# Two weight blocks split earlier, in the spatial weight's rooms, and one group's request moved ahead of three stores

## The chip, the cores and the metric

The kernel runs on one core of one Trainium2 chip. The metric is device time in microseconds (us) for one execution. Each shown time is one execution of the whole program.

## The reference

Inputs are q, k, v of shape 4 x 8 x 768 x 64 (batch, heads, positions, head width). First a retention layer with a decay per head, then a gated MLP with a spatial weight, everything in float32:

```python
gamma = 1.0 - 2.0 ** (-5.0 - np.arange(H))
for t in range(S):
    state = gamma * state + np.einsum('bhd,bhe->bhde', k[:, :, t], v[:, :, t])
    y[:, :, t] = np.einsum('bhd,bhde->bhe', q[:, :, t], state) / np.sqrt(D)
x = y.transpose(0, 2, 1, 3).reshape(B, S, H * D)          # 4 x 768 x 512
h = np.maximum(x @ w_in, 0.0)                             # w_in: 512 x 1024
u, v = h[..., :512], h[..., 512:]
v_n = (v - mean(v)) / np.sqrt(var(v) + 1e-06)             # over the last axis
v_s = np.einsum('ts,bsd->btd', w_spatial, v_n) + b_spatial[None, :, None]
out = (u * v_s) @ w_out                                   # w_out: 512 x 512
```

The weights w_in and w_out arrive as 64-bit floats; w_spatial is 768 x 768.

## The kernel before

**Tiling.** The positions of each batch make six groups of 128, so 24 groups in all, numbered from 0 (groups 0 to 5 are batch 0). Group g is three DMA requests: two for its values and queries (tile qv) and one for its keys (kk). Both tiles have three buffers, so group g can be requested when the last reader of group g - 3 is done. Retention runs per group: scores `s`, outputs `x`, then `xf` (scaled, VectorE), `xh` (rounded high part, ScalarE) and `xl` (the rest, GpSimd). The MLP of a batch has six tiles V (one per group: products `v`, activation `vr`, statistics `bst`, `mv`, `rs`, `nb`, normalised `vnh`), and eight units (four column blocks j, two halves of the positions). A unit has products `u`, activation `ur`, the spatial product `sp`, the gate `t` (two VectorE steps, L542 and L543), `gh` (ScalarE), `gl` (GpSimd), and the output product `o`. Accuracy comes from products of high and low parts, so each float32 weight needs a high and a low half.

**Weight blocks.** The 64-bit weights are twelve blocks of 128 x 512, split on the chip. Blocks 0 to 3 are V's weight, 4, 5, 6 and 8 are u's weight for j = 0, 1, 2, 3, and blocks 7, 9, 10, 11 are w_out for j = 0 to 3. A split is: `split_top` (ScalarE, L184, writes a), `split_exponent` (two VectorE steps on a, L190, L192), `split_sign` (two VectorE steps, L201 writes f, L205 writes a), `split_low` (one VectorE step, L210), `split_high` (ScalarE, L213, the high half), `split_residue` (two GpSimd steps, L140 and L227, the low half). In the profile a and f are `da` and `df`, or `room` where they lie in the spatial weight's buffers: four rooms of the pool tag "wsp" serve as a for blocks 0 to 5 before the last three tiles of the spatial weight (wst3 to wst5) take them.

**Order.** Nothing here is reordered freely: `START`, `FIRST` and the strings after them are lists of words that `emit` carries out one by one (L34 to L52), and each engine works off its own instructions in that order. Letters: a top, c the three VectorE steps (c60 is block 6, step 0), H high, R residue, C all of a split, V products of a V tile, r its activation, s statistics, w power, n bias, N normalise, u and D products u, P spatial product, O output product, I a whole unit, S scores and state of a group, Z scores alone, X its output, G request of a group, L request of a weight block, K request of a spatial tile, W its split. All requests and stores are issued by one queue, SyncE's (SP), which handles them strictly in turn; an issue whose buffer is not free holds up all behind it.

**The place of the change** is batch 0's MLP, about 56 to 125 us of the profile. PSUM tag "m" has two buffers, shared by `v`, `u` and `sp`; a buffer is handed on in the order in which its last reader was written in the list. In `START` the word `u1` stands ahead of `r4`, and `u0` ahead of `r5`; so V tile 5 gets the buffer of u1 and the first `sp` that of u0. Blocks 6 and 7 are split only in `FIRST` (`C6 P0 C7 P1`), after tile 5 of V.

Of the kernel before, what the change touches and what calls it, by code (L numbers as in the profile page):

```python
# [9 lines left out]
F32 = mybir.dt.float32  # L10
# [28 lines left out]
)  # L39
FIRST = (  # L40
    "C6 P0 C7 P1 D2 O0 C8 C9 P2 G7 Z5 D3 O1 C10 P3 S6 D4 O2 G8 C11 X6 S7 I4 G9 X7 S8 W0 G10 I5 X8 "
    "S9 W1 G11 I6 X9 S10 W2 G12 V0 V1 I7 X10 S11 G13 N0 V2 N1 V3 N2 X11 G14 V4 N3 V5 N4 O7 N5"
)
SECOND = (
    "S0 I0 W3 X0 S1 G3 I1 W4 X1 S2 G4 I2 W5 X2 S3 G5 I3 X3 S4 G6 I4 X4 S5 G7 I5 X5 G8 "
# [10 lines left out]
STAGED = {i: (("vnh", "vnl")[i // 3], i % 3) for i in range(6)}  # L56
STAGED |= {i: ("vnl", i - 8) for i in range(8, 11)}
UNIT_BLOCKS = 2
WARM_UP = 10


@with_exitstack
def tile_retention_gmlp(
# [17 lines left out]
    P = 128  # L81
# [8 lines left out]
    DM = KT * P  # L90
# [8 lines left out]
    mpool = ctx.enter_context(tc.tile_pool(name="mlp", bufs=2))  # L99
# [75 lines left out]
    def sp_tile(dtype, name):  # L175
        return mpool.tile([P, 2, HALF], dtype, tag="wsp", name=name, bufs=2 * (NC // 2) + 1)

    rooms = [sp_tile(F32, f"room{i}").rearrange("p i c -> p (i c)")[:, :DM] for i in range(4)]
# [15 lines left out]

    def split_sign(i):
        a, _, parts = halves[i]
        f = mpool.tile([P, DM], F32, tag="u", name=f"df{i}", bufs=3)[:, :]
        halves[i][1] = f
        ai, fi = a.bitcast(I32), f.bitcast(I32)
        tc.keep_in_program_order(  # L200
            nc.vector.scalar_tensor_tensor(  # L201
                fi, parts[:, :, 1], -0x40000000, ai, ALU.bitwise_and, ALU.bitwise_or
            )
        )
        tc.keep_in_program_order(nc.vector.tensor_scalar(ai, fi, -0x800000, None, ALU.bitwise_and))  # L205
# [9 lines left out]
    def split_residue(i):  # L215
        hi, lo, _ = doubles[i]
        a, f, _ = halves.pop(i)
        if i < UNIT_BLOCKS:

# [12 lines left out]
    def split_double(i):  # L232
        for step in (split_top, split_exponent, split_sign, split_low, split_high, split_residue):
            step(i)
# [339 lines left out]
    def item(b, i):  # L574
# [40 lines left out]
        "u": lambda b, g, n: mlp_u(0, *units[n]),  # L615
        "a": lambda b, g, n: split_top(n),
        "c": lambda b, g, n: (split_exponent, split_sign, split_low)[n % 10](n // 10),
        "H": lambda b, g, n: split_high(n),
        "R": lambda b, g, n: split_residue(n),
# [9 lines left out]
    wps = ps_o.tile([P, DM], F32, tag="o", name="wps")  # L629
    for i in range(WARM_UP):  # L630
        nc.tensor.matmul(wps, wz[:, :P], wz, start=True, stop=True)
# [84 lines left out]
```

## Time and profile before

| | |
|---|---|
| times of three runs | 417.2, 421.4, 425.0 us (median 421.4) |
| the profiled execution | 420.8 us, its span 418.8 us |
| TensorE busy | 387.2 us, 92% of the span |
| VectorE, GpSimd, ScalarE busy | 53%, 37%, 31% |
| mean granted TensorE clock | 0.976 |

TensorE is the busy engine. The rows to look for are therefore the stretches where it is not busy, or where its granted clock is below 1: each row of a wait names what released the engine, and each row of the windows gives busy time per engine and the clock (PEclk).

### The profile page before, as it was taken

Reading aid. Unit: us, or ns where it says so; the run is one execution under the profiler, and the core shown is the slowest. Engines: PE = TensorE matmul, PEld = TensorE weight load, DVE = VectorE, ACT = ScalarE, POOL = GpSimd, SP = SyncE. Lnnn points to the kernel's source line nnn. Section 1 sums busy time; section 2 is a strip of 40 time slices with the busy share of each in tenths; the row PEclk is TensorE's granted clock in tenths of the full one; section 3 lists DMA queues with packets and bytes.
Section 4 is the critical chain, followed back from the end, with each engine's and each line's share of the span. In section 5 each row is a group of like instructions: output and inputs, shape, how many; then the busy total and the mean of one; then the engine's idle time right before and its main releaser. Section 6 shows DMA issues by size and latency. Waiting matters only on the chain.

```text
span 418.8 us, 9002 instructions
## 1 busy us (share of the span) xinstructions
PE 387.2 (92%) x3748; PEld 327.6 (78%) x3748; DVE 222.0 (53%) x505; ACT 131.8 (31%) x242; POOL 156.3 (37%) x152
## 2 busy tenths in 40 slices
PE   4877999599939999999999999999999999999996
PEld 1546776367728777799999988899998988999995
DVE  0999763886925676557666224575553245212122
ACT  2464534222230233643223223721113135411212
POOL 0476851766640445225444412334442321011010
PEclk9989999779987999999999999999999999999999
DMA  7979959100071333323346410133302000200202
GB/s 181 320 241 257 295 182 294 43 2 2 2 226 52 102 102 99 103 77 103 107 121 189 130 38 2 68 102 108 105 2 77 0 2 0 77 0 1 77 1 75
DMA packets 14392, 41.47 MB, mean 99 GB/s; under 512 B 2320, under 2 KB 2704, under 8 KB 14352
## 3 DMA queue, kind: packets, MB, share of 16 engines
q1 hardware_dynamic: 14352, 40.91, 32.7%
q8 instruction: 29, 0.48, 0.5%
q14 instruction: 11, 0.09, 0.1%
HBM read 34.61 MB, written 6.29 MB: 98 GB/s over the span
## 4 chain that ended last, share of the span: by engine, by line
PE 84%; DMA 7%; POOL 3%; SPq 2%; DVE 2%; issue 1%; ACT 1%; POOLq 0%; DVEq 0%; ACTq 0%
PE sp L132 25%; PE u L132 17%; PE o L132 16%; PE v L132 15%; PE x L132 5%; PE s L132 5%; DMA qv<-in_qv_dram 4%; DMA kk<-in_k_dram 3%; SPq L137 2%; POOL qv L276 1%; POOL xl L140 1%; DVE xf L398 1%; POOL df L140 0%; POOL wout_w L227 0%; POOL winu_w L227 0%
## 5 line engine op out<-in xcount | busy, mean ns | idle before, releaser
L140 POOL TENSOR_TENSOR gl<-t,gh 128x384 fp32r<-128x384 f32 x31 | 32.4, 1044 | 132.1 <-ACT gh L544 74.5
L132 PE MATMUL u<-xh,winu_w 128*128 128x384 f32 x256 | 73.8, 351 | 2.4 <-POOL winu_w L227 2.4
L132 PE MATMUL o<-wout_w,gh 128*128 128x512 f32 x192 | 62.8, 408 | 3.4 <-POOL wout_w L227 3.4
L542 DVE TENSOR_TENSOR t<-sp,bsp_t 128x384 f32<-128x384 f32 (+1 forms) x34 | 18.0, 533 | 83.1 <-PE sp L132 83.1
L132 PE MATMUL v<-winv_w,xh 128*128 128x512 f32 x192 | 60.5, 397 | 0.6 <-ACT ur L511 0.6
L276 POOL TENSOR_TENSOR qv<-qv,vd_t 64x512 f32<-64x512 f32 x48 | 52.1, 1086 | 22.1 <-DMA qv<-in_qv_dram 20.3
L132 PEld LDWEIGHTS u<-xh,winu_w 128*128 128x128 f32 x256 | 47.9, 192 | 4.5 <-POOL winu_w L227 2.7
L132 PE MATMUL sp<-wsp_h,vnl 128*128 128x384 f32 x144 | 48.2, 335 | 0.0
L132 PE MATMUL sp<-wsp_h,vnh 128*128 128x384 f32 x144 | 48.2, 335 | 0.0
L132 PE MATMUL sp<-wsp_l,vnh 128*128 128x384 f32 x144 | 48.2, 335 | 0.0
L544 ACT CAST gh<-t 128x384 fp32r<-128x384 f32 (+1 forms) x34 | 16.6, 493 | 94.1 <-DVE t L543 93.8
L132 PEld LDWEIGHTS o<-wout_w,gh 128*128 128x128 f32 x192 | 36.6, 192 | 11.0 <-POOL wout_w L227 4.0
L132 PE MATMUL u<-xl,winu_w 128*128 128x384 f32 x128 | 43.8, 342 | 0.0
L140 POOL TENSOR_TENSOR xl<-xf,xh 128x512 fp32r<-128x512 f32 x24 | 31.4, 1309 | 31.5 <-ACT xh L415 31.4
L132 PEld LDWEIGHTS v<-winv_w,xh 128*128 128x128 f32 x192 | 35.4, 188 | 8.5 <-ACT ur L511 0.9
L320 DVE TENSOR_TENSOR qv<-s,mask_t 64x256 f32<-64x256 f32 x96 | 40.3, 419 | 1.6
L132 PE MATMUL s<-qv,kk 64*64 64x64 f32 x1296 | 26.9, 230 | 15.2 <-DMA kk<-in_k_dram 15.2
L132 PEld LDWEIGHTS s<-qv,kk 64*64 64x64 f32 x1296 | 23.5, 141 | 20.7 <-issue 11.8
L398 DVE SCALAR_TENSOR_TENSOR xf<-x,qg_t,qd_t 128x128 f32<-128x128 f32 x96 | 27.1, 342 | 23.0 <-PE x L132 22.9
L132 PE MATMUL o<-wout_w,gl 128*128 128x512 f32 x96 | 38.4, 400 | 0.0
L132 PE MATMUL v<-winv_w,xl 128*128 128x512 f32 x96 | 37.7, 392 | 0.8 <-POOL xl L140 0.8
L462 DVE BATCH_NORM_STATS2 bst<-vr 128x6 f32<-128x512 f32 x24 | 16.6, 692 | 33.1 <-ACT vr L455 33.1
(71 smaller groups left out, 569.5 us busy)
## 6 DMA issues: line engine op xcount, KB each, us to landing
qv<-in_qv_dram SPq DMA_DIRECT2D x48, 256.0 KB, 4.9
kk<-in_k_dram SPq DMA_DIRECT2D x24, 512.0 KB, 5.7
out_dram<-ot SPq DMA_DIRECT2D x23, 256.0 KB, 2.0
wst<-in_w_sp_dram SPq DMA_DIRECT2D x6, 384.0 KB, 8.2
raw<-in_w_inv_dram SPq DMA_DIRECT2D x4, 512.0 KB, 9.2
raw<-in_w_inu_dram SPq DMA_DIRECT2D x4, 512.0 KB, 9.6
raw<-in_w_out_dram SPq DMA_DIRECT2D x4, 512.0 KB, 6.8
bsp_t<-in_b_sp_dram SPq DMA_DIRECT2D x1, 384.0 KB, 10.9
```

The costliest lines, as they stand in the source:

```text
L132: ins = nc.tensor.matmul(out, lhs, rhs, start=start, stop=stop, skip_group_check=shared)
L137: tc.keep_in_program_order(nc.sync.dma_start(dst, src))
L140: return eng.tensor_tensor(out, whole, high.bitcast(F32), ALU.subtract)
L276: tc.keep_in_program_order(nc.gpsimd.tensor_tensor(w, w, vd, ALU.mult))
L320: keep(nc.vector.tensor_tensor(m[r][ROWS[r], i], ts[i][col, 0], mk, ALU.mult))
L398: nc.vector.scalar_tensor_tensor(xf[:, hp], t[:, hp].rearrange("p i c -> p (i c)"), qg_t[:, c, hp : hp + 1], qd_t[:, hp], ALU.mult, ALU.mult,)
L462: keep(nc.vector.bn_stats(st, norm[b, c][0]))
L542: nc.vector.tensor_tensor(t[:, c], pp[:, c], bsp_t[:, tc_], ALU.add)
L544: nc.scalar.copy(gh[:, c], t[:, c])
```

## The change

The change edits the two lists and the room for one tile. Nothing is computed differently: the same instructions run on every engine, 353 rows on VectorE and 228 on ScalarE in both.

```diff
     "t41 k41 l2 j5 y40 h3 t50 w1 y41 k50 s0 l3 V2 E4 w0 n1 h4 n0 c40 N1 l4 y50 r2 c41 V3 N0 s2 H4 "
-    "c42 y51 w2 r3 V4 E5 R4 L8 L9 L10 L11 K3 K4 K5 s3 h5 n2 u1 r4 l5 N2 s4 w3 V5 w4 n3 N3 n4 N4 u0 "
-    "r5 s5 w5 n5 N5"
+    "c42 y51 w2 r3 V4 E5 R4 L8 L9 L10 L11 s3 h5 a6 n2 r4 l5 N2 c60 u1 s4 w3 V5 w4 n3 N3 n4 N4 c61 "
+    "c62 H6 a7 c70 r5 u0 s5 R6 w5 n5 N5 c71 c72 H7 R7"
 )
 FIRST = (
-    "C6 P0 C7 P1 D2 O0 C8 C9 P2 G7 Z5 D3 O1 C10 P3 S6 D4 O2 G8 C11 X6 S7 I4 G9 X7 S8 W0 G10 I5 X8 "
-    "S9 W1 G11 I6 X9 S10 W2 G12 V0 V1 I7 X10 S11 G13 N0 V2 N1 V3 N2 X11 G14 V4 N3 V5 N4 O7 N5"
+    "C8 P0 G7 P1 G8 K3 K4 K5 C9 D2 O0 Z5 P2 D3 O1 C10 P3 S6 D4 O2 C11 X6 G9 S7 I4 X7 S8 W0 G10 I5 "
+    "X8 S9 W1 G11 I6 X9 S10 W2 G12 V0 V1 I7 X10 S11 G13 N0 V2 N1 V3 N2 X11 G14 V4 N3 V5 N4 O7 N5"
 )
...
+
+FAR = [6, 7]
...
     def split_sign(i):
         a, _, parts = halves[i]
-        f = mpool.tile([P, DM], F32, tag="u", name=f"df{i}", bufs=3)[:, :]
+        if i in FAR:
+            f = rooms[i - FAR[0]]
+        else:
+            f = mpool.tile([P, DM], F32, tag="u", name=f"df{i}", bufs=3)[:, :]
```

Blocks 6 and 7 are now split among the last two tiles of V; their a lies in rooms 2 and 3, their f in rooms 0 and 1, so wst3 to wst5 are requested after them (K3 to K5 moved into `FIRST`, behind groups 7 and 8). The activations r4 and r5 stand ahead of u1 and u0. The second spatial product P2 follows the scores Z5 instead of preceding them. The request of group 9 (G9) stands right behind X6. Line numbers below 60 grow by 2 and those after the new lines by 5.

The queue of SP, from the last weight block on (wst: spatial weight, qv and kk: a group, out: the stores of batch 0's first half). Before:

```order
L137 DMA wst3_737<-in_w_sp_dram 128x768
L137 DMA wst4_739<-in_w_sp_dram 128x768
L137 DMA wst5_741<-in_w_sp_dram 128x768
L137 DMA qv7_938<-in_qv_dram 64x1024 x2
L137 DMA kk7_939<-in_k_dram 128x1024
L137 DMA qv8_1084<-in_qv_dram 64x1024 x2
L137 DMA kk8_1085<-in_k_dram 128x1024
L569 DMA out_0_dram<-ot0_0_0_1202 128x512
L569 DMA out_0_dram<-ot0_0_1_1208 128x512
L569 DMA out_0_dram<-ot0_0_2_1214 128x512
L137 DMA qv9_1217<-in_qv_dram 64x1024 x2
L137 DMA kk9_1218<-in_k_dram 128x1024
```

Changed:

```order
L139 DMA qv7_862<-in_qv_dram 64x1024 x2
L139 DMA kk7_863<-in_k_dram 128x1024
L139 DMA qv8_881<-in_qv_dram 64x1024 x2
L139 DMA kk8_882<-in_k_dram 128x1024
L139 DMA wst3_886<-in_w_sp_dram 128x768
L139 DMA wst4_888<-in_w_sp_dram 128x768
L139 DMA wst5_890<-in_w_sp_dram 128x768
L139 DMA qv9_1122<-in_qv_dram 64x1024 x2
L139 DMA kk9_1123<-in_k_dram 128x1024
L574 DMA out_0_dram<-ot0_0_0_1203 128x512
L574 DMA out_0_dram<-ot0_0_1_1209 128x512
L574 DMA out_0_dram<-ot0_0_2_1215 128x512
```

Groups 7 and 8 went ahead of the three spatial tiles, and group 9 went ahead of the three stores.

ScalarE, from the last `xh` of batch 0 (group 5) to the last `vnh`. Before:

```order
L415 CAST xh3_578<-xf5_724 128x4x128
L511 ACTIVATE ur0_1_0_765<-u0_1_0_752 128x384
L455 ACTIVATE vr0_4_767<-v0_4_711 128x512
L485 ACTIVATE vnh0_448<-vr0_2_673,nb0_2_750,rs0_2_694 128x512
L485 ACTIVATE vnh0_448<-vr0_3_709,nb0_3_792,rs0_3_745 128x512
L485 ACTIVATE vnh0_448<-vr0_4_767,nb0_4_795,rs0_4_773 128x512
L511 ACTIVATE ur0_0_0_811<-u0_0_0_798 128x384
L455 ACTIVATE vr0_5_813<-v0_5_778 128x512
L485 ACTIVATE vnh0_448<-vr0_5_813,nb0_5_822,rs0_5_817 128x512
```

Changed:

```order
L420 CAST xh3_578<-xf5_724 128x4x128
L186 ACTIVATE room2_90<-raw6_86 128x512
L460 ACTIVATE vr0_4_747<-v0_4_711 128x512
L490 ACTIVATE vnh0_448<-vr0_2_673,nb0_2_745,rs0_2_694 128x512
L516 ACTIVATE ur0_1_0_766<-u0_1_0_753 128x384
L490 ACTIVATE vnh0_448<-vr0_3_709,nb0_3_789,rs0_3_739 128x512
L490 ACTIVATE vnh0_448<-vr0_4_747,nb0_4_792,rs0_4_770 128x512
L218 CAST winu_w_83<-room0_88 128x512
L186 ACTIVATE room3_91<-raw7_87 128x512
L460 ACTIVATE vr0_5_802<-v0_5_775 128x512
L516 ACTIVATE ur0_0_0_817<-u0_0_0_804 128x384
L490 ACTIVATE vnh0_448<-vr0_5_802,nb0_5_828,rs0_5_821 128x512
```

Each `vr` now stands ahead of the `ur` beside it, and block 6's top and high half and block 7's top lie between them.

VectorE, around the statistics of V tile 5 (bst0_5). Before:

```order
L462 BN_STATS bst0_5_815<-vr0_5_813 128x6
L463 BN_AGGR mv0_5_816<-bst0_5_815 128x2
L464 TENSOR_SCALAR rs0_5_817<-mv0_5_816 128x1
L474 TENSOR_SCALAR nb0_5_822<-mv0_5_816,rs0_5_817 128x1
L190 TENSOR_SCALAR da6_825<-da6_825 128x512
L542 TENSOR_TENSOR t0_0_0_843<-sp0_0_0_836,bsp_t_79 128x384
L192 TENSOR_SCALAR da6_825<-da6_825 128x512
L543 TENSOR_TENSOR t0_0_0_843<-t0_0_0_843,ur0_0_0_811 128x384
L201 SCALAR_TENSOR_TENSOR df6_829<-raw6_86,da6_825 128x512
L205 TENSOR_SCALAR da6_825<-df6_829 128x512
L210 SCALAR_TENSOR_TENSOR da6_825<-raw6_86,da6_825 128x512
L190 TENSOR_SCALAR da7_850<-da7_850 128x512
```

Changed:

```order
L206 SCALAR_TENSOR_TENSOR room0_88<-raw6_86,room2_90 128x512
L210 TENSOR_SCALAR room2_90<-room0_88 128x512
L215 SCALAR_TENSOR_TENSOR room2_90<-raw6_86,room2_90 128x512
L192 TENSOR_SCALAR room3_91<-room3_91 128x512
L194 TENSOR_SCALAR room3_91<-room3_91 128x512
L467 BN_STATS bst0_5_819<-vr0_5_802 128x6
L468 BN_AGGR mv0_5_820<-bst0_5_819 128x2
L469 TENSOR_SCALAR rs0_5_821<-mv0_5_820 128x1
L479 TENSOR_SCALAR nb0_5_828<-mv0_5_820,rs0_5_821 128x1
L206 SCALAR_TENSOR_TENSOR room1_89<-raw7_87,room3_91 128x512
L210 TENSOR_SCALAR room3_91<-room1_89 128x512
L215 SCALAR_TENSOR_TENSOR room3_91<-raw7_87,room3_91 128x512
```

Block 6 and the first two steps of block 7 went ahead of these statistics (block 6's own first two steps even ahead of tile 4's), and the rest of block 7 stands right behind them. The gate `t0_0_0` of the first unit then follows the two exponent steps of block 8.

## The prediction

> **What bounds the kernel now.** I read the waits of TensorE first, then the chain that ended last, then the windows. TensorE is busy for 92% of the span, so time can come only from where it stands still or runs at a lower clock. Its waits between 56 and 135 us (total, times, longest):
>
> ```profile
> PE s L132 <- DMA kk<-in_k_dram: 6.8, 1, 6.8
> PE o L132 <- POOL wout_w L227: 3.4, 1, 3.4
> PE u L132 <- POOL winu_w L227: 2.4, 1, 2.4
> PE v L132 <- ACT ur L511: 0.6, 1, 0.6
> PE sp L132 <- ACT ur L511: 0.6, 1, 0.6
> ```
>
> All five are in batch 0's MLP. Two are for the low halves of blocks 6 (winu_w) and 7 (wout_w), two for a PSUM buffer that `ur` gives back, and one for the keys of group 9. The chain gives start, length and work:
>
> ```profile
> 58.40 2.12 PE u L132 x12
> 61.08 3.02 PE v L132 x12
> 66.79 4.40 PE sp L132 x12
> 92.52 0.62 PE s L132 x32
> 97.52 3.87 PE sp L132 x12
> 101.39 1.09 PE s L132 x64
> 102.48 2.28 PE u L132 x12
> 104.77 2.08 PE o L132 x9
> 106.84 1.23 PE x L132 x32
> 115.31 2.09 PE o L132 x9
> 117.40 1.11 PE x L132 x32
> 119.77 5.27 DMA kk<-in_k_dram
> 125.28 2.10 PE s L132 x62
> 127.38 3.49 PE u L132 x12
> ```
>
> The last rows show what a wait costs beyond itself: after it, `s` took 2.10 us and `u` 3.49 us, against 1.09 and 2.28 at 101.39 and 102.48. The windows say why (length; busy us and instructions of PE, PEld, DVE, ACT, POOL; PEclk, DMA share, GB/s):
>
> ```profile
> 20.74:24.15 3.41, 1.34 (x22) 0.89 (x20) 3.32 (x8) 2.38 (x6) 1.83 (x2) 1.00 1.04 351
> 24.15:27.56 3.41, 3.41 (x18) 1.29 (x19) 3.38 (x7) 1.24 (x3) 3.00 (x4) 0.50 1.02 264
> 37.80:41.22 3.42, 2.04 (x38) 1.78 (x39) 3.24 (x9) 1.58 (x3) 1.19 (x2) 1.00 1.04 241
> 75.35:78.76 3.41, 1.02 (x6) 0.97 (x6) 3.38 (x4) 0.00 (x0) 2.31 (x2) 1.00 0.02 7
> 78.76:82.17 3.41, 2.23 (x7) 1.62 (x6) 2.27 (x6) 2.08 (x4) 2.14 (x2) 0.50 0.01 2
> 82.17:85.58 3.41, 1.17 (x3) 0.98 (x4) 3.31 (x4) 0.64 (x2) 2.19 (x2) 0.50 0.00 0
> 85.58:89.00 3.42, 3.42 (x9) 2.50 (x8) 3.27 (x4) 0.57 (x1) 2.92 (x2) 0.50 0.02 5
> ```
>
> The clock changes at steps of 3.41 us. A step with TensorE busy for 1.34 or 1.02 us is followed by clock 0.50; one with 2.04 us is not. It is back after a fully busy step, so the two gaps at 75 and 81 us halve the clock for three steps, to 89.00.
>
> **Part one: blocks 6 and 7 earlier, and the buffers.** From 58.40 to 101.39 the profile took 42.99 us. TensorE's work there at full clock is u 2 x 2.12, v 3.02, sp 4 x 3.87, u 2 x 2.28, o 2 x 2.08 and s 0.62: 32.08 us. So 10.91 us are the most that this part can give. They are 0.56 and 0.57 before `v` and `sp` (from chain rows to chain rows: 61.08 - 58.40 - 2.12, and likewise at 66.79), 0.53 inside the first `sp` (4.40 - 3.87), the waits of 2.4 and 3.4, and 3.4 of half clock, the remainder.
>
> The two buffer waits: V tile 5 now takes the buffer that `vr` of tile 4 frees, the first `sp` that of `vr` of tile 5. Each is a step done long before the next product asks, if ScalarE and VectorE keep up. They have the room:
>
> ```profile
> 61.55 0.69 DVE L462 BATCH_NORM_STATS2 bst<-vr 128x6 f32<-128x512 f32 x1 [3.71 <-ACT vr L455]
> 67.26 0.69 DVE L462 BATCH_NORM_STATS2 bst<-vr 128x6 f32<-128x512 f32 x1 [3.73 <-ACT vr L455]
> 69.40 0.81 ACT L485 ACTIVATE vnh<-vr,nb,rs 128x512 f32<-128x512 f32 x1 [2.17 <-DVE nb L474]
> ```
>
> A block is five VectorE steps, 0.43 + 0.43 + 0.69 + 0.43 + 0.69 = 2.7 us when GpSimd is idle, so two blocks want 5.3 of the 7.4 us in these two gaps. But GpSimd is not idle. Rows with it:
>
> ```profile
> 81.68 0.43 DVE L190 TENSOR_SCALAR da<-da 128x512 f32<-128x512 f32 x1 [1.07 <-ACT da L184]
> 72.49 0.69 DVE L201 SCALAR_TENSOR_TENSOR df<-raw,da 128x512 int32<-128x512 int32 x1
> 75.12 1.49 DVE L190 TENSOR_SCALAR da<-da 128x512 f32<-128x512 f32 x1
> 76.65 1.37 DVE L192 TENSOR_SCALAR da<-da 128x512 int32<-128x512 int32 x1
> 57.44 1.29 POOL L227 TENSOR_TENSOR winu_w<-df,room 128x512 fp32r<-128x512 f32 x1
> 74.65 1.68 POOL L140 TENSOR_TENSOR df<-df,winu_w 128x512 f32<-128x512 f32 x1 [0.45 <-DVE da L205]
> 76.41 1.33 POOL L227 TENSOR_TENSOR winu_w<-df,da 128x512 fp32r<-128x512 f32 x1
> ```
>
> L190 at 75.12 ends 0.28 us after the GpSimd step of 74.65 to 76.33, and L192 at 76.65 ends 0.28 after that of 76.41 to 77.74: such a step runs between two of GpSimd's, not beside them. I walk the new order with that rule.
> - Block 6's exponent steps start at 57.9 and, behind two GpSimd steps (57.44, and the `xl` that ends near 60), are done at 60.4. Tile 4's statistics follow at once, earlier than 61.55.
> - Block 6's other steps fit before 63.7. Block 7's exponent steps meet block 6's two residue steps and end at 66.8; tile 5's statistics start then. Before, `vnh` was done 2.95 us after their start (67.26 to 70.21); with nothing else in that chain now, it is done at 69.4 to 69.7. The first `sp`, which starts at 58.40 + 2.12 + 3.02 + 2.12 = 65.66, asks for it 5/6 x 3.87 later, at 68.9: 0.5 us of wait stay.
> - Second `sp` ends at 73.9. Block 6 is long done, so `u` has no wait: it ends at 76.2.
> - The first gate `t` stands behind the rest of block 7 and block 8's exponent steps, which run between block 7's residues: it starts at 73.2, is done at 74.8, `gh` at 75.3. On GpSimd, `gl` stands behind block 8's first residue step, which waits for block 8's high half and loses turns to VectorE: 75.7 to 76.9; `gl`, again between VectorE steps, ends at 78.4. The first `o` has used `gh` up by 76.7: 1.7 us of wait.
> - From there blocks 8 and 9 are done (79.6, 85.2) before `u` and the second `o` ask (84.5, 86.8), and TensorE runs to the end of the fourth `sp`. Block 10 (near 93) is asked for at 96.
>
> What stays is 0.5 + 1.7 = 2.2 us, so part one gives 10.9 - 2.2 = **8.7 us**. Bounds: 10.9 if nothing stays; below, the GpSimd waits of 2.4 and 3.4 could stay whole with their half clock of 3.4, leaving only the two buffer waits, 1.1. I take the walk, because it is made of rows. The 1.7 us lie between the two kinds of step seen above (1.34 busy of 3.41 lowers the clock, 2.04 of 3.42 does not): 3.41 - 1.7 leaves 1.7 busy. If that lowers it, one step at half speed costs another 1.7.
>
> The Trainium skill ("TensorE: Matmul & The Clock Gate", under "What's actually happening") says that the clock falls after at least one idle window of about 3.4 us. By that the stall would cost itself alone; the row at 20.74 disagrees, since 1.34 us of work did not save the clock.
>
> Moving P2 behind the scores costs nothing: `s` (0.62 us) is work that must be done anyway.
>
> **Part two: group 9 ahead of the stores.** SP's rows:
>
> ```profile
> 116.65 1.78 SPq L569 DMA_DIRECT2D out_dram<-ot  x3
> 118.60 1.12 SPq L137 DMA_DIRECT2D qv<-in_qv_dram  x2
> 119.77 0.58 SPq L137 DMA_DIRECT2D kk<-in_k_dram  x1
> ```
>
> The stores could go only when the first half's outputs were ready, and group 9 stood behind them. Its buffers are free once `x` of group 6 is done, at 106.84 + 1.23 = 108.07. From its first issue to the landing of kk passed 119.77 + 5.27 - 118.60 = 6.4 us. So it lands 6.4 us after `x6` ends, and the products that need it come s 1.09, u 2.28, sp 3.87, o 2.09, x 1.11 = 10.4 us after that end: 4 us to spare. The wait of 6.8 goes, and with it the half clock after it: 2.10 - 1.09 + 3.49 - 2.28 = 2.2. That is **9.0 us**. Bounds: 9.0 above, since TensorE has nothing else to lose there; below 6.8, if some other pause keeps a slow step. Next in line is group 10, behind the three stores and behind `x7`; it has the same 10.4 us against 6.4. The issues that were moved behind block 7's residues, wst3 to wst5, go out by about 73; the landing of such a tile
>
> ```profile
> wst<-in_w_sp_dram SPq DMA_DIRECT2D x3, 384.0 KB, 8.0
> ```
>
> puts them at 81, and the half that reads them began at 111.44, now about 103. That cover is 20 us; without it each us would show. Groups 7 and 8 go earlier, to no one's harm: nothing else is asked for before 81.
>
> **Sum.** 420.8 (the profiled execution) - 8.7 - 9.0 = **403.1 us**. The median shown is 421.4, so this execution is 0.6 below it; the runs spread from 417.2 to 425.0.
>
> **Rivals.**
> - *The clock falls again.* `gl` is later than I walk it (2.4 us or more, as the wait for winu_w was), the clock halves for one to three steps, and with 3.4 lost as before part one gives 8.7 - 0.7 - 3.4 = 4.6 or less: 407.2 and up. For it: VectorE's column in the windows has 3.27 to 3.38 of 3.41 us busy in three of the four steps from 75.35 on, so it is short of room there. Against: 5.3 us of its work leave that stretch. Where the wait reaches the 3.4 and the clock both gaps' price, only the buffer waits are gained, and the time is 410.7.
> - *Nothing stays.* 10.9 + 9.0 give 400.9. For it: my walk gives every conflict to the waiting side.
> - *The change does half of what it says*: group 9's request finds its buffers still read, by the state steps of group 6 or by SP standing before K3 to K5, and arrives as late as now. Then part two is nothing and the time is 412.1. Against: 10 us between its free buffers and the issue.
> - *Slower than before.* The half clock feeds on itself: after the first stall TensorE never has a fully busy step until group 9, because each `o` waits for its own block. By the walk TensorE has some 34 us of work without a break from 78 to 112; at half clock it would take 34 more. It becomes slower than before once more than 17.7 us of work run at half clock. Price if all does: 420.8 - 17.7 + 34 = 437. Against: the row at 85.58 shows one full step, and blocks 8 to 10 come ahead of need above.
>
> **How the numbers follow.** My forecast has a chance of 0.60, the clock rival 0.20, nothing stays 0.13, half of it 0.05, slower 0.02. The range: below, 400.9 less two us for the spread of runs, 399; above, most of the clock rival, 410. A measurement can tell about 2% from no change, 8.4 us. The forecast, the clock rival and "nothing stays" all lie beyond that (under 413); half of it straddles the bound: faster 0.94, within 2% 0.04, slower by over 2% 0.02.
>
> **What would show it.** Right: no wait of `s` for kk near 109; the rows `v` and first `sp` follow `u` with no idle; `u` no longer waits for winu_w; one wait of `o` for `gl` (GpSimd L142) of 1 to 2 us near 77; PEclk 1.00 from 56 to 130. Wrong: a wait for wout_w or winu_w of over 2 us, PEclk 0.50 in any slice there, a wait of `sp` for wst3, or a span above 409.

## The result, and the profile after

The changed kernel took 404.17 us (median of four runs, 401.85 to 405.4), the kernel before beside it 423.2 us (four runs, 417.2 to 425.81): a ratio of 0.963, with a 95% interval of 0.952 to 0.975. The ratios here and below compare fast executions alone (of the kernel before, those within 1.5% of its fastest), so they are not those of the two medians. It is faster, one us above the forecast of 403.1 and inside the range. The profiled execution took 405.03 us, its span is 403.2 us and its mean granted clock 0.995 (before 420.8, 418.8 and 0.976). The page of the profile counts the same instructions on these engines in both: 3748 on TensorE, 505 on VectorE, 242 on ScalarE and 152 on GpSimd.

TensorE's waits in the changed kernel between 56 and 130 us (total, times, longest):

```profile
PE o L134 <- POOL gl L142: 1.4, 1, 1.4
PE sp L134 <- ACT vnh L490: 1.3, 1, 1.3
```

Of five waits two are left, and both are new: the first `o` for `gl`, and the first `sp` for the last `vnh`. The waits for winu_w, wout_w, `ur` (twice) and kk are gone.

To see where the time came from, I cut each execution at two marks of TensorE that have the same work between them in all kernels here: the first `u` after V tile 4, and the scores with state (`s`, 64 instructions) of group 6 and of group 9. **A** is the stretch from the first mark to group 6, **B** the one from there to group 9. The windows of the kernel before (length; PE, PEld, DVE, ACT, POOL busy; PEclk, DMA share, GB/s):

```profile
58.23:101.32 43.09, 36.12 (x159) 25.38 (x157) 27.20 (x44) 13.27 (x23) 22.02 (x19) 0.88 0.39 116
101.32:137.84 36.52, 29.72 (x376) 23.97 (x375) 19.70 (x42) 8.31 (x16) 15.49 (x15) 0.91 0.28 81
```

And of the changed kernel:

```profile
59.79:94.68 34.89, 32.23 (x159) 23.26 (x157) 27.57 (x44) 12.52 (x22) 22.58 (x20) 1.00 0.51 144
94.68:122.18 27.50, 27.50 (x376) 21.83 (x375) 19.93 (x42) 8.32 (x16) 15.28 (x14) 1.00 0.38 107
```

Read the first two numbers of each row. A fell by 43.09 - 34.89 = 8.20 us: idle time went from 6.97 to 2.66 (length less PE busy), and the busy time itself from 36.12 to 32.23, as PEclk rose from 0.88 to 1.00. B fell by 36.52 - 27.50 = 9.02: 6.80 of idle time and 2.22 of half clock, and now TensorE stands still nowhere in it. The rest of the span, from B's end on, is 280.96 us before and 281.02 after. So the whole gain lies in A and B, 17.22 us. The two spans differ by only 15.6, because the changed kernel's execution came to the first mark 1.56 us later, at 59.79 instead of 58.23. TensorE's instructions ahead of that mark stand in the same order in both lists. On other engines the edit reaches into the last us before it (the requests for wst3 to wst5 went out at 57.60 before, block 6's top step runs at 58.91 now), and TensorE waits for neither. The last section comes back to the start.

The chain that ended last (start, length, work) has, at the place where `s` and `u` had taken 2.10 and 3.49 us:

```profile
101.43 1.09 PE s L134 x64
102.52 2.28 PE u L134 x12
104.80 3.87 PE sp L134 x12
108.67 2.09 PE o L134 x9
110.76 1.08 PE x L134 x32
111.84 1.09 PE s L134 x64
112.93 2.28 PE u L134 x12
```

Every step has its length at full clock, and each begins where the one before it ends. SP's rows say why no `s` waits any more:

```profile
68.33 6.82 SPq L139 DMA_DIRECT2D wst<-in_w_sp_dram  x3
101.52 1.11 SPq L139 DMA_DIRECT2D qv<-in_qv_dram  x2
102.67 0.58 SPq L139 DMA_DIRECT2D kk<-in_k_dram  x1
110.01 2.15 SPq L574 DMA_DIRECT2D out_dram<-ot  x3
112.33 1.12 SPq L139 DMA_DIRECT2D qv<-in_qv_dram  x2
```

Group 9 is asked for at 101.52, when group 6's outputs are done, and no longer behind the three stores, which now go out at 110.01.

### The profile page after: what moved, and what is told of

The parts are those of the page before. It is cut to its first block, busy times and chain, and to the rows that moved or that the text cites. A ratio compares the mean times of both kernels' runs of the same rounds, so it can differ in the third digit from the quotient of the medians.

```text
span 403.2 us, 9004 instructions
## 1 busy us (share of the span) xinstructions
PE 380.9 (94%) x3748; PEld 324.0 (80%) x3748; DVE 223.3 (55%) x505; ACT 131.7 (33%) x242; POOL 156.3 (39%) x152
## 4 chain that ended last, share of the span: by engine, by line
PE 78%; DMA 5%; POOL 4%; DVE 2%; issue 1%; ACT 0%; SPq 0%; POOLq 0%; DVEq 0%; ACTq 0%
PE sp L134 24%; PE o L134 16%; PE u L134 16%; PE v L134 12%; PE x L134 5%; PE s L134 5%; DMA qv<-in_qv_dram 5%; POOL xl L142 1%; POOL df L142 1%; POOL winu_w L232 1%; POOL rs L474 1%; POOL qv L281 0%; POOL gl L142 0%; DVE bst L467 0%; DVE df L206 0%
## 5 line engine op out<-in xcount | busy, mean ns | idle before, releaser
L142 POOL TENSOR_TENSOR gl<-t,gh 128x384 fp32r<-128x384 f32 x31 | 32.6, 1053 | 118.0 <-ACT gh L549 68.9
L134 PE MATMUL u<-xh,winu_w 128*128 128x384 f32 x256 | 72.3, 345 | 0.0
L134 PE MATMUL o<-wout_w,gh 128*128 128x512 f32 x192 | 61.1, 399 | 0.0
L134 PEld LDWEIGHTS u<-xh,winu_w 128*128 128x128 f32 x256 | 46.7, 188 | 1.8
L134 PE MATMUL u<-xl,winu_w 128*128 128x384 f32 x128 | 42.9, 335 | 0.0
L134 PEld LDWEIGHTS o<-wout_w,gh 128*128 128x128 f32 x192 | 35.7, 188 | 6.8
L134 PE MATMUL sp<-wst,vnh 128*128 128x384 f32 x96 | 32.5, 488 | 1.3 <-ACT vnh L490 1.3
```

Of the source, the lines that this page charges most:

```text
L134: ins = nc.tensor.matmul(out, lhs, rhs, start=start, stop=stop, skip_group_check=shared)
L142: return eng.tensor_tensor(out, whole, high.bitcast(F32), ALU.subtract)
```

## The experiments

The change's A and B came out the same within a tenth in both of its profiles (34.89 and 34.84, 27.50 twice), the total did not, since the start moves it. So the table gives the stretches of each profiled execution. Where waits lower the clock, A repeats less well: the same order gave 43.09 before and 42.27 in e1.

| kernel | first mark at | A | B | rest | span |
|---|---|---|---|---|---|
| before | 58.23 | 43.09 | 36.52 | 280.96 | 418.8 |
| the change | 59.79 | 34.89 | 27.50 | 281.02 | 403.2 |
| e1: request alone | 58.89 | 42.27 | 27.50 | 280.94 | 409.6 |
| e2: blocks alone | 59.54 | 34.83 | 37.57 | 280.96 | 412.9 |
| e3: activations alone | 57.15 | 39.91 | 36.91 | 280.93 | 414.9 |
| e9: residue late | 60.36 | 34.91 | 27.50 | 280.93 | 403.7 |
| e7: gate first | 55.70 | 33.38 | 27.50 | 280.92 | 397.5 |
| e11: e7 and e9 | 57.44 | 33.42 | 27.53 | 281.01 | 399.4 |
| e4: activations back | 59.55 | 34.39 | 27.53 | 281.03 | 402.5 |
| e5: no rooms | 58.56 | 33.24 | 27.50 | 280.90 | 400.2 |
| e8: statistics and gate first | 63.06 | 31.69 | 27.50 | 280.95 | 403.2 |
| e10: the change again | 61.80 | 34.84 | 27.50 | 280.96 | 405.1 |

The kernels differ from one another in order or buffers only.

**e1: part two alone.** On the kernel before, only the request is moved.

```diff
-X6 S7 I4 G9 X7
+X6 G9 S7 I4 X7
```

> The kernel before with only group 9's request moved ahead of the three stores. Two stretches are read from the trace: A from the first u after V tile 4 to the first scores with a state step (before 43.1 us, the change 34.9), B from there to the third later scores (before 36.5, the change 27.5). My theory, two independent terms: A stays 43.1, B is 27.5, the wait of s for kk is gone and the clock after it is 1.00; 9.0 us off, ratio 0.979. Rival, the request gains only together with the earlier blocks, because group 6's buffers are still read: the wait for kk stays above 3 us, B above 33, ratio 0.99 or more.

413.1 us (411.11 to 415.72) against 423.25, a ratio of 0.980 (0.973 to 0.987): faster, by an amount on both sides of the 2% that the prediction set as its bound. B is 27.50, as in the change. Its waits between 56 and 135 us:

```profile
PE o L132 <- POOL wout_w L227: 2.6, 1, 2.6
PE u L132 <- POOL winu_w L227: 2.4, 1, 2.4
PE sp L132 <- ACT ur L511: 0.6, 1, 0.6
PE v L132 <- ACT ur L511: 0.6, 1, 0.6
```

The four waits of A stay, the one for kk is gone. So the request alone brings all of B. A is 0.8 us shorter than before although its order is the same: the wait for wout_w is 2.6 and not 3.4.

**e2: part one alone.** On the changed kernel, the request goes back behind the stores.

```diff
-X6 G9 S7 I4 X7
+X6 S7 I4 G9 X7
```

> The change with group 9's request put back behind the stores. My theory: A is 34.9, B is 36.5 with the wait of 6.8 us for kk and the slow clock after it; 8.2 us off, ratio 0.98. Rival, the landing of group 9 is fixed by something that does not move with batch 0's MLP: then the wait for kk grows by what A gains, B is about 44 and the ratio 1.00.

416.51 us (414.83 to 419.52), a ratio of 0.987 (0.981 to 0.993): faster, but by less than 2%. Waits and the row of the timeline:

```profile
PE s L134 <- DMA kk<-in_k_dram: 7.6, 1, 7.6
PE o L134 <- POOL gl L142: 1.4, 1, 1.4
PE sp L134 <- ACT vnh L490: 1.2, 1, 1.2
```

```profile
119.09 2.10 PE L134 MATMUL s<-qv,kk 64*64 64x64 f32 x64 [7.56 <-DMA kk<-in_k_dram]
```

A is 34.83, that of the change, so part one doesn't need part two. B came out at 37.57, one us above the kernel before: the wait is 7.56 instead of 6.80, and half clock adds 2.51 instead of 2.22. The theory's A was right, its gain in total a little too large.

**e3: V's activations ahead of u's, alone**, on the kernel before.

```diff
-n2 u1 r4 l5 N2 s4 ... N4 u0 r5 s5
+n2 r4 l5 N2 u1 s4 ... N4 r5 u0 s5
```

> The kernel before with only the two activations of V ahead of the two of u. My theory: the waits of v and sp for ur (0.57 each) go, and since the splits of blocks 6 and 7 start behind V's last tile, they start 1.1 us earlier too: A is 42.0. Rival, the waits for the low halves swallow it: the wait of u for winu_w grows from 2.4 to about 3.5, A stays 43.1.

416.89 us in one run. A is 39.91, 3.2 us less: both the theory and its rival had missed. Its waits, and VectorE's steps for block 6:

```profile
PE s L132 <- DMA kk<-in_k_dram: 7.1, 1, 7.1
PE o L132 <- POOL wout_w L227: 4.0, 1, 4.0
PE u L132 <- POOL winu_w L227: 1.2, 1, 1.2
```

```profile
66.44 0.43 DVE L190 TENSOR_SCALAR da<-da 128x512 f32<-128x512 f32 x1 [1.50 <-ACT da L184]
66.90 0.43 DVE L192 TENSOR_SCALAR da<-da 128x512 int32<-128x512 int32 x1
67.36 0.69 DVE L201 SCALAR_TENSOR_TENSOR df<-raw,da 128x512 int32<-128x512 int32 x1
68.66 0.42 DVE L205 TENSOR_SCALAR da<-df 128x512 int32<-128x512 int32 x1
```

The two waits for `ur` are gone, as said, and the wait for winu_w is halved as well: the edit also made the first three of block 6's five steps stand together ahead of the gate, where GpSimd is idle. So this is not the activations alone: a word of the list moved more than itself. What the activations bring in the change is looked at in e4.

**e9: block 6's residue behind the statistics of V tile 5.** It tests the first new wait: if VectorE's two steps for block 7 are slow because they run between GpSimd's two, they get short when GpSimd's come later.

```diff
-r5 u0 s5 R6 w5 n5 N5 c71
+r5 u0 s5 w5 n5 N5 R6 c71
```

> The change with the power step of V tile 5 ahead of block 6's two residue steps on GpSimd; VectorE's order is the same. If VectorE's two exponent steps of block 7 are long (1.19 and 1.37 us in the change) because GpSimd's residue steps run, they take 0.43 each here, the statistics of tile 5 start 1.5 us or more earlier, and the wait of sp for vnh (1.3) is gone; the wait of o for gl may grow, A between 33.5 and 36. Rival, they are long by themselves or wait for their data: over 1.0 us each, and the wait of sp stays above 1 us.

405.52 us in one run. The steps in the changed kernel, on GpSimd and on VectorE:

```profile
65.45 1.44 POOL L142 TENSOR_TENSOR room<-room,winu_w 128x512 f32<-128x512 f32 x1 [1.75 <-ACT winu_w L218]
66.97 1.33 POOL L232 TENSOR_TENSOR winu_w<-room,room 128x512 fp32r<-128x512 f32 x1
```

```profile
65.99 1.19 DVE L192 TENSOR_SCALAR room<-room 128x512 f32<-128x512 f32 x1 [0.25 <-ACT room L186]
67.22 1.37 DVE L194 TENSOR_SCALAR room<-room 128x512 int32<-128x512 int32 x1
68.51 0.68 DVE L467 BATCH_NORM_STATS2 bst<-vr 128x6 f32<-128x512 f32 x1
```

In e9:

```profile
66.35 0.43 DVE L192 TENSOR_SCALAR room<-room 128x512 f32<-128x512 f32 x1 [0.25 <-ACT room L186]
66.81 0.43 DVE L194 TENSOR_SCALAR room<-room 128x512 int32<-128x512 int32 x1
67.15 0.69 DVE L467 BATCH_NORM_STATS2 bst<-vr 128x6 f32<-128x512 f32 x1
```

1.19 and 1.37 us became 0.43 and 0.43, and `sp` no longer waits for `vnh`. The steps in the changed kernel both end 0.29 us after GpSimd's (66.89 and 68.30): they take turns. The Trainium skill ("SBUF — State Buffer", under "Who interferes with whom") says that VectorE in its two-port modes, which `tensor_scalar` can enter, shares a pair of ports with GpSimd, and that who issues first has it for the whole instruction. These rows agree, and give the price, 0.76 and 0.94 us a step.

But A stayed at 34.91, within the 33.5 to 36 that was expected. The waits only moved:

```profile
PE o L134 <- POOL gl L142: 1.7, 1, 1.7
PE u L134 <- DVE t L547: 1.0, 1, 1.0
```

This run also answers what the prediction left open on the clock. Its clock fell at 22.70 and rose at 29.52 us. Steps of 3.413 us counted on from there (19 of them lie between the changes at 24.15 and 89.00 in the kernel before) put the wait for `gl` into the step from 77.31 to 80.72. TensorE is busy for 1.71 us of that step, and PEclk in the step behind it is 1.00. So here 1.71 us of work kept the clock, where 1.34 did not in the kernel before.

**e7: the first gate ahead of block 8.** It tests the second new wait, `o` for `gl`.

```diff
-C8 P0 G7 P1
+P0 C8 G7 P1
```

> The change with the first spatial product's word ahead of block 8's split, so that on VectorE both steps of the first gate stand ahead of block 8's exponent steps, and on GpSimd gl stands ahead of block 8's residue. My theory: the wait of o for gl (1.37 us in the change) is made by that order; it goes, the wait of sp for vnh (1.3) stays, A is 33.5. Rival: the wait moves on, as a wait of u for winu_w (block 8, now later) or of o for wout_w, and A stays 34.9.

399.41 us in one run, A 33.38 (33.5 expected). One wait is left:

```profile
PE sp L134 <- ACT vnh L490: 1.3, 1, 1.3
```

So `gl` was late because it and its gate stood behind block 8's steps on VectorE and GpSimd. Its execution is 5.6 us shorter than the change's: 1.5 of that is A, and 4.1 is the start (55.70 against 59.79).

**e11: e7 and e9 together.**

> The change with both: the gate ahead of block 8's split, and the power step of tile 5 ahead of block 6's residue. With the residue alone late, A was 34.9 as in the change, because u then waited 1.0 us for the gate t and o 1.7 for gl. My theory: these two waits hang on the gate's place, so here both pairs go and A is 32.2 to 33.0 (full-speed work is 32.1); time 401 to 403 with the change's start. Rival: VectorE and GpSimd have no room left for all of it and a wait of 1.5 us or more stays at u or o; A 34 or more.

401.13 us, A 33.42, between what theory and rival had said: `sp` no longer waits for `vnh`, but the residue of block 7 comes later with that of block 6, and `o` waits for it:

```profile
PE o L134 <- POOL wout_w L232: 1.5, 1, 1.5
```

**e4: the activations as before, blocks and request as in the change.**

```diff
-a6 n2 r4 l5 N2 c60 u1 s4 ... c70 r5 u0 s5
+a6 n2 u1 r4 l5 N2 c60 s4 ... c70 u0 r5 s5
```

> The change with the activations of u ahead of those of V again, blocks 6 and 7 still split early. The scheduler now also puts the first gate ahead of block 8's exponent steps, so the wait for gl is 0 to 0.5. My theory: V tile 5 and the first sp wait for ur again, 0.6 us each, and tile 4's statistics and all behind them come 1.1 us later; A is 34.9 + 1.1 - 1.4 = 34.6. Rival, from the run with the activations alone (A 3.2 us shorter, not 1.1): the order of the activations is worth about 3 us, and A is 36.5 or more.

404.37 us in one run, A 34.39 (34.6 expected). Its waits:

```profile
PE sp L134 <- ACT vnh L490: 0.7, 1, 0.7
PE sp L134 <- ACT ur L516: 0.6, 1, 0.6
PE v L134 <- ACT ur L516: 0.6, 1, 0.6
```

The waits for `ur` are back, and TensorE, held up for them, waits less for `vnh`. But the edit moved `gl` too: it runs at 76.72, ahead of block 8's residue at 78.80, as in e7, so the wait for it is gone as it is there. Beside the change (34.89) the activations' place seems to bring nothing. Beside e7 (33.38), which also has `gl` early, their old place costs 1.0 us. What they bring in the change by themselves is not shown.

**e5: `df6` and `df7` from their own pool again.**

```diff
-FAR = [6, 7]
+FAR = []
```

> The change with f of blocks 6 and 7 in the tile that it had before (three buffers shared with ur) and not in the rooms; the order of the list is the same, and the scheduler puts gl ahead of block 8's residue. My theory: the rooms are not what brings the time; f of block 7 waits for block 6's residue, which is done by then, and A is 33.5 to 35. Rival: five tiles want three buffers, block 7 or 8 or ur waits for a gate to free one, a wait of over 1.5 us shows at u or o for winu_w or wout_w, and A is 37 or more.

402.2 us in one run, A 33.24 (33.5 to 35 expected):

```profile
PE sp L134 <- ACT vnh L490: 0.7, 1, 0.7
PE o L134 <- POOL wout_w L232: 0.3, 1, 0.3
```

The rooms for f are not what brings the time (a stays in its rooms here). Without them `gl` stood ahead of block 8's residue, as in e7, and A is that of e7 within 0.14 us.

**e8: the first gate ahead of block 8 and the statistics of tile 5 ahead of block 7.** Both new waits are aimed at, without moving block 6's residue.

```diff
-c70 r5 u0 s5 R6 w5
+r5 u0 s5 c70 R6 w5
...
-C8 P0 G7 P1
+P0 C8 G7 P1
```

> The change with two further moves in the list: on VectorE block 7's exponent steps stand behind the statistics of V tile 5 (GpSimd keeps block 6's residue early), and the first gate stands ahead of block 8's split. The gate alone gave A 33.4, with the wait of sp for vnh (1.3) left; the late residue took that wait away but gave 1.5 back at o, since block 7's residue came later. My theory: here the residue is not late, so neither wait is there, A is 32.2 to 32.9, and the time is 2.0 to 2.7 us below that of the change in the same job (ratio to before 0.947 to 0.955). Rival: block 7 comes later by its two moved steps, o waits for wout_w 1 us or more, and A is 33.4 or above.

**e10: the change once more**, beside e8.

> The change itself, timed again beside the kernel before. Theory: A 34.9, B 27.5, the rest from the third later scores to the end 281.0, in a ratio of 0.955 to 0.963. Rival, that the times of the first measurement hung on the start of the program: then A + B + rest stays and the ratio leaves 0.95 to 0.975.

e8 took 403.12 us (six runs, 400.93 to 405.02), the change 405.28 (six runs, 402.83 to 407.0), the kernel before 422.11: ratios of 0.956 (0.951 to 0.961) and 0.961 (0.955 to 0.966). The change came out as expected of e10, in its stretches and in its ratio. The two intervals overlap, so the totals alone don't settle it (2.16 us between the medians); the stretch A tells them apart, 31.69 us against 34.84 and, in the first profile of the change, 34.89. It is below the 32.2 to 32.9 that were expected of e8, while its ratio is just above the 0.947 to 0.955. The window of A in e8:

```profile
63.06:94.75 31.69, 31.69 (x159) 23.42 (x157) 25.29 (x44) 12.63 (x22) 20.93 (x18) 1.00 0.53 154
```

TensorE is busy for all of it at full clock, so in this stretch no wait is left that an order of the other engines could take away.

## Why the prediction was right

**Part one: 8.20 us where 8.7 was said.** The working list was right in kind: the two waits for blocks 6 and 7 went with their half clock, and the two stalls left are the two that the walk named. Their sizes were off: `sp`'s wait was 1.28 us and not 0.5, `o`'s 1.37 and not 1.7, together 2.65 instead of 2.2. The first is the term that was mis-sized. The walk's own times (`vnh` done at 69.4 to 69.7, asked for at 68.9) allow 0.5 to 0.8, and it took the lower end. Moved by the 1.56 us that the first mark is later here, block 7's exponent steps should have ended at 68.36 and ended at 68.59, and `vnh` should have been done by 71.26 at the latest:

```profile
70.57 0.81 ACT L490 ACTIVATE vnh<-vr,nb,rs 128x512 f32<-128x512 f32 x1 [3.12 <-DVE nb L479]
```

It was done at 71.38, and TensorE asked for it at 70.16 and not at 70.46. So the rule of turns itself was right (e9), and the miss is made of a few tenths at both ends. The second wait was shorter than said because the first was longer: TensorE came to `gl` 0.51 us later than in the walk so moved, `gl` only 0.13.

The most that part one could give was set too low: 10.91 was counted from chain rows, and e8, with no wait left, gives 43.09 - 31.69 = 11.40. And the tenths in 8.20 are not firm: from e1's A, the same order as before, the gain would be 7.38. e2 shows part one alone at the same A. e5 shows that the rooms for f are not its source, and e4 that most of the gain stays with the activations in their old place. What remains as the source is the earlier place of the blocks: the two waits for their low halves are gone. Undoing that by itself was not tried, nor was taking back the swap of P2 and Z5 or the earlier requests of groups 7 and 8.

**Part two: 9.02 us where 9.0 was said**, from the same two terms, 6.80 of wait and 2.22 of half clock. e1 shows it alone. That it fits to a hundredth says little, as both figures are read from the same execution before: where the request stood behind the stores in e2 and e3, B was 37.57 and 36.91. wst3 to wst5 went out until 75.15 and not 73, and the half that reads them began at 104.80 (in the chain above); no wait for them showed, so the cover held.

**The sum.** 17.22 us were gained in the two stretches where 17.7 were forecast. The profiled execution is 1.9 us above 403.1: 0.5 from these stretches, 1.56 from the start, 0.06 from the rest, less 0.17 outside the span. That the median came within about one us of the forecast is in part luck, since the start alone moved executions by several us.

**The rivals.** *The clock falls again* is out: PEclk is 1.00 in both windows. Its two stalls cost little more than themselves: 2.65 us of waits, and 3.20 us in A beside e8, which has none. These two do not decide between the Trainium skill's rule of an idle window and the row at 20.74, where 1.34 us of work did not save the clock: neither stall leaves less than 2 us of work in a step of 3.41, and a step with 2.04 kept the clock before too. e9 narrows it to between 1.34 and 1.71 us. *Nothing stays* failed by 2.65 us, but e8 shows that an order without waits exists. *The change does half of what it says* is out: the request goes out at 101.52. *Slower* needed half clock, and there was none.

## What to carry to other kernels

Read the gain from the stretch that a change touches, between two marks with the same work: here the stretch repeats within a tenth where the clock stays at 1.00 (34.89 and 34.84 us, and 34.83 in e2), while the start moves the total by several us. With half clock in it, one and the same order gave lengths 0.8 us apart. A request behind a store in one queue waits for the store's data; what it costs is the wait and the slow clock after it, and a request whose buffers are free earlier belongs ahead of the store. Where VectorE and GpSimd take turns, the place of a GpSimd step sets how long VectorE's steps are, so the step that TensorE waits for should come first, and the others go beside no one or behind it.

## What was not expected of the hardware

**The start.** The first mark came between 55.70 and 63.06 us, with TensorE's instructions ahead of it in one order of the list. TensorE's largest waits for the keys and for `qv` differ there, in the changed kernel and in e10, which is the same kernel (whole execution, total, times, longest):

```profile
PE s L134 <- DMA kk<-in_k_dram: 8.5, 3, 6.4
PE total L134 <- ACT qv L306: 5.1, 2, 3.2
```

```profile
PE s L134 <- DMA kk<-in_k_dram: 12.6, 3, 8.6
PE total L134 <- ACT qv L306: 2.9, 3, 1.5
```

Their sum is 13.6 and 15.5 us; that makes 1.9 of the 2.0 us between these two starts (59.79 and 61.80). Over all executions it does not explain the whole: e8 has 14.8 and starts at 63.06, at a mean granted clock of 0.84 up to the mark, the change at 0.97. Of the 3.27 us that e8 starts later than the change, 1.11 are idle time of TensorE (16.38 and 15.27 up to the mark) and 2.16 longer busy time (46.68 and 44.52). Why the keys and `qv` come at other times in each execution was not tested and stays open.

**One order, two lengths.** A was 43.09 us before and 42.27 in e1, in the same order, with PEclk 0.88 and 0.92. TensorE's busy time is nearly alike (36.12 and 36.16); what differs is idle time, the wait for wout_w above all (3.4 and 2.6). In e1 the half clock begins earlier in the `u` before that wait, so TensorE comes to `o` later. The Trainium skill ("TensorE: Matmul & The Clock Gate", under "What's actually happening") says that the clock's window runs free of the kernel's start; a step that falls elsewhere on the same stalls would do this, and the profile before showed changes at steps of 3.41 us. No run moved the start on purpose, so this is not shown.
